# Pooled attention and a gated feed-forward on one core: weight words joined without ScalarE, a score tile's short product first, more engine choices, another order

## The chip, the core and the metric

The program runs on one core of a Trainium2 chip. A core has a matrix engine (TensorE, PE in the profile), a vector engine (VectorE, DVE), an activation engine (ScalarE, ACT), a general engine (GpSimd, POOL) and a queue that issues the transfers here (SyncE, SP). Each engine takes its instructions in the order in which they were recorded, and waits at an instruction until all that this one needs is done. The metric is the time of one execution on the device in microseconds (us).

## The reference, cut to what matters

```python
# q, k, v: (4, 8, 1152, 64) float32
q_pool = q.reshape(B, H, S // 2, 2, D).mean(axis=3)              # 576 pooled queries
scores = scale * np.matmul(q_pool, k.transpose(0, 1, 3, 2))      # 576 x 1152 for each head
scores = scores - np.max(scores, axis=-1, keepdims=True)
attn = np.exp(scores)
attn = attn / (np.sum(attn, axis=-1, keepdims=True) + 1e-09)
attn_out = np.matmul(attn, v)
x = attn_out.transpose(0, 2, 1, 3).reshape(B, 576, 512)          # the heads side by side
h = np.maximum(x @ w_in, 0.0)                                    # 512 -> 1024
conv_out = sum(conv_w[t] * shifted(h, t - 1) for t in range(3))  # over neighbouring tokens
out = (h * 1.0 / (1.0 + np.exp(-conv_out))) @ w_out              # 1024 -> 512
```

`w_in`, `conv_w` and `w_out` arrive as 64-bit floats. The kernel reads each as two 32-bit words and puts a 32-bit float together on the chip.

## The kernel before, in words

The 32 heads go in 16 pairs. A pair's 576 pooled queries are cut into four blocks of 128 and one of 64. For a block of 128 and one head of the pair there is a **score tile** of 128 queries by 1152 keys; the two heads share one tile for the block of 64. That makes 9 tiles for a pair and 144 in all.

A tile takes this way. `scores` (line 459) makes it on PE in three products, each with one half of PE's rows (64 of 128, since a head has 64 values): `main` 0 and 1 are 512 keys each and lie in different halves, `main` 2 is the 128 keys in the middle and lies in the half of `main` 0. The operand `qt` is the pair's queries, `qd` the same queries turned to the other half of the partitions. DVE takes the row maximum (`top`, 471), ACT the exponential with its row sum (`expo`, 476); DVE or ACT scale and invert the sum (489, 493, 499). Then a head goes one of two ways. For most heads ACT or POOL writes the high half of the weights in 16 bits (`high`, 518 on POOL and 523 on ACT), DVE the low half (`low`, 526), and a transposing transfer (539) turns both. For the seven heads in `X32`, POOL, DVE or ACT scale the row (`norm`, 557 and 561), PE turns it (575), and ACT brings it back from PSUM (`keep`, 580). Score tiles `s` have two buffers and the PSUM tiles `a` of all other products have two.

`values` (605, 611) multiplies the turned weights with v; ACT brings the result back (`keep`, 621), ACT or POOL splits off a high half (627, 629), DVE the low half (634). When the four pairs of a batch have their part, `feed` makes the 1024 hidden rows: products on PE (695), `relu` on ACT (701), the first tap on ACT or POOL (708, 712), two more taps on DVE (719), `tanh` on ACT (725), the gate on DVE (729). `second` makes the output product (902, 908, 914), ACT brings it back (928) and SP stores it.

The weights are put together in 17 pieces (`weights`: 8 of `w_in`, 8 of `w_out`, all 128 x 512, and a small one of 24 columns for `conv_w`). A piece takes, in a chain: load (987), absolute value on ACT (`size`, 991), `clamp` on DVE (995), three bit operations on DVE (`bits`, 1004, 1009, 1013), the low words made into scaled floats on ACT (`rest`, 1019), a product on DVE (`join(0)`, 1026) and a sum on POOL or DVE (`join(1)`, 1028); for `w_in` ACT adds up absolute values (1047). The query pairs are added up by `sum_q` (303), kept by `keep_q` (306) and turned by `turn_q` (310).

What stands where is written out by hand in three tables. `ORDER` names all tasks in one list over all engines; each engine's own order is that list with the others' tasks left out. `SWAPPED` names the tasks that go to their second engine (`alt`) instead of the first, and `SLOTS` gives each buffer its slot. There is no scheduler at run time. A task can change engine only where it has an `alt`.

Of the kernel before, what the change touches and what calls it, by code (L numbers as in the profile page):

```python
# [88 lines left out]
def unpack(words):  # L89
# [5 lines left out]
hZcZcXaac1c4c0c5c6c7cYh0auc2bNc3abacaddcaededdc8afdbh3h1daagdfahc9h2dtaih4aviiajawh5aEaxdsaybOilh6h7azifijh8aA  # L95
igdgdhibikaBihh9imaCdiiDaFdjindwaGicaHiAioiaaIaDaJiddyipakiBiqdldxdzdmixiEivaKdNdMieaLitiFiyiualiraMiCamiSanao
iGaNiHapaOdQaqd6iViwardSiTasiPiWiIatisaYiXiQdAiJaPjadniRiUaQdoaRaSiYdRiZaTiLjbi7aUiziKaZiNdpaVdqjva0jca1aWi8dT
iMd7jyi0a2i9jdjea3iOi3jwjia4i1i4i2jfjzjjjxi5a5i6jNjAjgjljBaXjQdrjmbijCa6dujneaa7jOjKa8ecjheddkdUjLjPdvdPjRjkbj
j5jDjSbkjIbljoj8j6a9ebjGbmjJetjMjEbnjHbabojrjTbbj7bpjUbcjFj9j2dBjVj3dCbdkabqj0knewbrkbdDkcbebEkqkkkoj1jsjYj4kd
jWkrjZkpkgbPkljXkFfGkhbFbfkikskmkGkebgkjdFk0kHbGktdGkudHdIkCesdJdKk3kIbHeydLexkDkSdOezkfkJk1bhkNkKbsk4kvk2kEkL  # L100
dEkOkTkPkQbtbIkRbJlik5bubvkMbyllk6k7ljlfbwkAlmk8kwkBkxkylgk9kzlkldbxlhlnlAbQlebzlDdVlolaeNbRlbbClpkWbSlBlxbKbT
dWbLbUlclylqlCdXbVlElvbMbDb5kXlzlFdZlSd0bAlGlHlVd1lPd2lIlTltlweQd3lWlulNlJb6lOb7lKlLb8lrlUb9calQcbmalXcclRlsmv
cdlYd4lZmbl0eRlMmcbWd5l5l1mwl7d8mdmyd9eSeAl2mebBl6l3mfmnl8eTmxmzmie7l9bXmgeedYeUmAmNbYmBmhbZmoefb0mQl4mCmOmDeg
mlmjmmmRmPmKmGmHb1mkmLmEb2mIm5mSehb3mMmJmTmUm6mFejmVm2m8ekb4elm7emm0eqmWencem9nnjpmXmpkUm1m3mYmrnajqm4ernoeojt
# [12 lines left out]
FstGFHtRFItPtzF8tHFJtQtStIF1F9gzFnGatJfIugF2fXF3tTFUuhtKtUtLF4tiF5tVtMtZGbuit0F6t2tWsat1GcFKt5GdF7FVgBtjGttXgD
FLFNGuGetYt3tkGvfOFWFuGwFOt6t4FPfPtNFvGxt7fQFXFMfRGfFQgCfSFYujtluxFRGgukfTult8GhuAfUuyGygEFwt9uBgSuaFxumFZFSub
uzGmF0uCfVuPfWGnuSuduQfZucGAGoueFyuDuEupuTuFuouUf5uGunGpuRvaufuIGzf6Gqu7uVFTGruWuqu0GBuLu8uHuJuMuXuKuNvbGVuOgo
u9uYFzu1gyGWFtvpu2Givcu3vqf7u5vHu4gUvrFAGjvIGku6vsvdf8GsveutvfvtvguZvuFBgVvvvhvwvigWFCvxuuFDvyG2FEGCFFGXg8GYvl  # L120
G3GDvJgaGZv2GEgbG4vmvnvKgcvAvLgdvjgev3vov5vkgfgXvzvPvDvFv6vMvEvGvBv4vQvNv7wgggvOvCG5wjvRwhGFgjv8JWg9vSgRvUv9GG
wdwkwagYwef9wlvTG6wiwbwuwfG7wmgpwnGlwIwowvvVGHwrwJwcwwHnwpGIG0G8GJwxwsHowKGOwyhbwzwtgqwWgrGKHpgsgtwLwAHqwBwXwF
vYwqGPG1wGwChcguGQwMhdgvGRHrwNwDHgwHvZgwwYwOgxxdHhwPGShegAxgxewEHiw5wZwTGLw0HjwQwUxhw1xfwVHuGTw2w6xrgGHkwRxiG9
GMxjHsGNxuwSfNHtHaxsHlHbHvxkHcxoxvw3HwxlxpxtgHxmHxxwHmxnHdxFgIHeGUxxHfxIgJxygKHAxGHBxzHCw4gPxHxqgLxAHDHyurxJgM
xCHExBgFvWxKxDxTuvw7xWxLxMw8xNxUw9usxQxEvXxXv0xVxRHFhqgNxYxOx7xaxZgOx0x8gTx1xPygx4uwv1x9x5xShsyryhyiyaHGyjyoht
x2IshugQhvypH0hHItybIuysIzycx3H1yqIvIeH2IAgZIwydHOIBytH3yfICyFH4IxIfyeJZyCIghJg0yux6HPIDyDHQIyyEg1yvyGHzywyzyQ
IhyxIlyAHRImyHyRyBIEyTIiySyIg2IFyJyNH7yUyyHSyKg3IGyOInziH5HHIoH8yLyVykyPH6Ijg4yWIHzjg5IIzkH9Iag6yMy4ylg7Ipy7yX
ymy5xbHIhLhay1yYy8hKHJIJzlzmy2znHKIqyZy3y9INIKy6IbzozDIcy0zaIdzbzGIOzfzEHLhNIrzFhpzgzrhMzHzczhIPzIIkynIQzdzRzs
# [43 lines left out]
def tile_pooled_attention_conv_gate_ffn(  # L172
# [262 lines left out]
    def softmax(o, d):  # L435
# [791 lines left out]
```

## Time and profile before

| | before |
|---|---|
| median of 3 runs | 635.98 us (635.82 to 636.93) |
| span of the profiled execution, first to last instruction | 633.9 us |
| what lies around the span (median less span) | 2.1 us |
| PE busy | 583.3 us (92%) |
| DVE busy | 575.9 us (91%) |
| ACT busy | 520.2 us (82%) |
| POOL busy | 159.6 us (25%) |

The page names no time of the profiled execution beside its span, so the median stands for it. Shares of the whole span are means over stretches with different limits; the rows further down cut the span into stretches. Only the time in which an engine waits, and what ends that wait, tells which engine sets the pace of a stretch. Times in the trace count from the span's start.

### The profile page before, as it was taken

The numbers are of one execution on the slowest core, as the hardware profiler recorded it, in microseconds if no ns is written. First come the engines' busy times: TensorE is split into PE (matmuls) and PEld (weight loads), VectorE is DVE, ScalarE is ACT, GpSimd is POOL, SyncE is SP. The second block draws the span as 40 slices with busy tenths as digits, with TensorE's granted clock in tenths as the row PEclk, the third lists the DMA queues.
The fourth block names the chain that finished last, engine by engine and source line by source line (L and its number), as shares of the span: only waits on it lengthen the run. The fifth ranks groups of instructions, "written<-read, shape, count | busy, mean of one in ns | idle before, by whom it ended". The sixth has DMA issues, their size and how long they took to land. (4 is left out here: it accounts for less than half of the span.)

```text
span 633.9 us, 11947 instructions
## 1 busy us (share of the span) xinstructions
PE 583.3 (92%) x4427; PEld 365.1 (58%) x4427; DVE 575.9 (91%) x948; ACT 520.2 (82%) x976; POOL 159.6 (25%) x166
## 2 busy tenths in 40 slices
PE   5679887898999899999999999999998999999997
PEld 3346554566665556546666666475665646566853
DVE  4999989999999999989998999999999999997771
ACT  5999989989998897879977899787869985775761
POOL 0332436533233312210212511202330122322210
PEclk7869989999999999999999999999999999999999
DMA  7788975847975599998989998999999898887601
GB/s 246 234 221 223 197 127 118 207 116 191 182 197 109 131 193 169 177 219 162 248 176 190 177 241 168 159 217 195 199 181 210 175 173 152 166 153 152 93 35 42
DMA packets 277386, 109.63 MB, mean 173 GB/s; under 512 B 264912, under 2 KB 266192, under 8 KB 277328
## 3 DMA queue, kind: packets, MB, share of 16 engines
q1 hardware_dynamic: 277328, 108.87, 83.3%
q8 instruction: 35, 0.57, 0.4%
q14 instruction: 23, 0.19, 0.1%
HBM read 37.77 MB, written 4.72 MB: 67 GB/s over the span
## 5 line engine op out<-in xcount | busy, mean ns | idle before, releaser
L476 ACT ACTIVATE p<-s,sm 128x1152 f32<-128x1152 f32 x144 | 175.2, 1217 | 41.2 <-DVE sm L471 18.8
L459 PE MATMUL s<-kt,qt 64*128 64x512 f32 (+3 forms) x704 | 189.0, 484 | 20.7 <-ACT p L476 16.5
L471 DVE TENSOR_REDUCE sm<-s 128x1 f32<-128x1152 f32 x144 | 193.1, 1348 | 7.3 <-PE s L459 6.9
L526 DVE SCALAR_TENSOR_TENSOR hl<-p,sm,hl 128x1152 f16<-128x1152 f32 (+1 forms) x116 | 167.0, 1449 | 4.3 <-POOL hl L518 2.4
L459 PEld LDWEIGHTS s<-kt,qt 64*128 64x128 f32 (+1 forms) x704 | 92.6, 178 | 124.3 <-issue 78.1
L459 PE MATMUL s<-kt,qd 64*128 64x512 f32 x256 | 147.3, 658 | 0.0
L518 POOL TENSOR_SCALAR hl<-p,sm 128x1152 f16<-128x1152 f32 (+1 forms) x52 | 72.1, 1388 | 230.1 <-DVE sm L499 145.8
L605 PE MATMUL a<-pt,v 128*64 128x256 f16 (+2 forms) x1566 | 119.8, 272 | 0.4 <-DVE v L399 0.4
L695 PE MATMUL a<-x,wi 128*128 128x257 f16 (+3 forms) x864 | 105.4, 274 | 3.6 <-ACT h L701 1.7
L605 PEld LDWEIGHTS <-v 128*64 128x64 f16 x1566 | 91.1, 110 | 10.2 <-issue 2.2
L695 PEld LDWEIGHTS <-wi 128*128 128x128 f16 x864 | 76.6, 98 | 30.3 <-issue 10.6
L523 ACT ACTIVATE hl<-p,sm 128x1152 f16<-128x1152 f32 (+1 forms) x64 | 79.4, 1249 | 12.3 <-DVE sm L499 9.1
L908 PE MATMUL a<-wo,g 128*128 128x512 f32 x160 | 74.7, 604 | 0.0
L719 DVE SCALAR_TENSOR_TENSOR g<-h,cw,g 128x255 f32<-128x255 f32 (+3 forms) x144 | 66.7, 482 | 4.1 <-ACT g L708 2.5
L575 PE MATMUL a<-ident,p 128*128 128x128 f32 (+1 forms) x315 | 49.1, 281 | 17.1 <-ACT pt L580 7.3
L611 PE MATMUL a<-pt,v 128*64 128x256 f32 (+1 forms) x252 | 64.1, 409 | 0.0
L575 PEld LDWEIGHTS a<-ident,p 128*128 128x128 f32 (+1 forms) x315 | 32.9, 144 | 31.1 <-ACT pt L580 10.1
L580 ACT ACTIVATE pt<-a 128x384 f32<-128x384 f32 (+2 forms) x98 | 44.6, 475 | 5.3 <-PE a L575 5.2
L701 ACT ACTIVATE h<-a,bs 128x257 f32<-128x257 f32 (+3 forms) x72 | 33.9, 472 | 14.3 <-PE a L695 9.4
L561 POOL TENSOR_SCALAR p<-p,sm 128x1152 f32<-128x1152 f32 (+1 forms) x20 | 28.1, 1408 | 69.0 <-DVE sm L499 42.9
L908 PEld LDWEIGHTS a<-wo,g 128*128 128x128 f32 x160 | 28.4, 190 | 28.8 <-issue 26.9
L611 PEld LDWEIGHTS a<-pt,v 128*64 128x64 f32 x252 | 33.4, 137 | 10.3 <-issue 0.7
(135 smaller groups left out, 648.8 us busy)
## 6 DMA issues: line engine op xcount, KB each, us to landing
qin<-in_q_dram SPq DMA_DIRECT2D x15, 640.0 KB, 4.6
kt<-in_k_dram SPq DMA_DIRECT2D x15, 576.0 KB, 5.0
vin<-in_v_dram SPq DMA_DIRECT2D x9, 576.0 KB, 4.4
g<-in_moe_w_in_dram SPq DMA_DIRECT2D x8, 512.0 KB, 4.6
w<-in_moe_w_out_dram SPq DMA_DIRECT2D x8, 512.0 KB, 4.2
out_dram<-o SPq DMA_DIRECT2D x16, 256.0 KB, 2.6
vin<-in_v_dram SPq DMA_DIRECT2D x7, 288.0 KB, 3.9
v<-in_v_dram SPq DMA_DIRECT2D x7, 288.0 KB, 4.1
```

Source lines behind the costliest of these rows:

```text
L459: nc.tensor.matmul(out=w, lhsT=f, rhs=kk, start=True, stop=True)
L471: nc.vector.tensor_reduce(out=sm[:, e:e + 1], in_=runs(st[e]), axis=AX.XY, op=ALU.max, negate=True)
L476: nc.scalar.activation(out=p.tile().rearrange("p (a n) -> p a n", a=2), in_=runs(st[e]), func=AF.Exp, bias=sm[:, e:e + 1], scale=1.0, accu ...
L518: eng.tensor_scalar(out=hl[rows, 0], in0=ps_[e][rows], scalar1=sm[rows, 6 + e:7 + e], scalar2=1.0, op0=ALU.mult, op1=ALU.mult,)
L523: nc.scalar.activation(out=hl[rows, 0], in_=ps_[e][rows], func=AF.Copy, scale=sm[rows, 6 + e:7 + e])
L526: nc.vector.scalar_tensor_tensor(out=hl[rows, 1], in0=ps_[e][rows], scalar=sm[rows, 6 + e:7 + e], in1=hl[rows, 0], op0=ALU.mult, op1=ALU.s ...
L575: nc.tensor.transpose(w[:, (i - a1) * nq:(i - a1 + 1) * nq], ps_[e][rows, i * P:(i + 1) * P], ident[rows, rows])
L605: nc.tensor.matmul(out=to, lhsT=o.v[:, e, c, vc:vc + D], rhs=o.pt[y, e][:, hl * NC + c, 0:n], start=(c == 0 and j == 0), stop=(c == NC - 1 ...
L611: nc.tensor.matmul(out=to, lhsT=o.v[:, e, c].bitcast(F32), rhs=p32.rearrange("p (a n) -> p a n", a=NC)[:, c, 0:n], start=(c == 0), stop=(c ...
L695: nc.tensor.matmul(out=w[:, 0:n], lhsT=wi[:, a, j, f * P:(f + 1) * P], rhs=x.x[:, c, s0:s0 + n], start=(i == 0 and j == 0), stop=(i == 2 a ...
L719: nc.vector.scalar_tensor_tensor(out=c, in0=h[:, t:t + tok], scalar=cw[:, f, t:t + 1], in1=c, op0=ALU.mult, op1=ALU.add)
L908: nc.tensor.matmul(out=w.tile(), lhsT=g[f // 4][:, f % 4, c:c + P], rhs=wo[:, f, :], start=(f == 0), stop=(f == FC - 1),)
```

## The change

**Weights.** `rest` is gone. `join(0)` now reads the low words itself, scales them and multiplies, in one instruction of DVE; ACT makes one conversion less for each of the 17 pieces. `clamp` may go to POOL.

**Score tiles.** `scores` makes the three products in the order `main` 2, 1, 0, so that the short one of 128 keys comes first and a long one of 512 last.

**Engine choices.** `turn_q`, the PSUM copies of `keep` in the softmax and in `values`, and `relu` may go to DVE instead of ACT.

**Order.** `ORDER`, `SLOTS` and `SWAPPED` are new throughout. Over the whole program POOL has 284 tasks in place of 160, DVE 862 in place of 888 and ACT 656 in place of 771; PE has the same 452.

```diff
 SWAPPED = """
-aiaMaWa6bqbAcdcNcWc8dcdqdwdKdQd4eaeoewe9fkfqfBf1gkgvgBgUhbhmhshJhUioixiGiYi0i7jfjpjBjDjKjVj2kkkCkIlflolqlxlGlY
+alaIaVa4bdbobybObWb4ccckcscAcNcPcTcUcVcYdhdCdVd7ete3fkfDgvgFg5hPh9iWi3i8jkjmjojEjGjIkckeklkrktkCkDkHk9lgltlHlJ
...
-        def turn_q(e, cols):
+        def turn_q(eng, e, cols):
             h, g = slice(D - D * e, P - D * e), slice(D * e, D * e + D)
+            if eng is not nc.scalar:
+                eng.tensor_scalar(
+                    out=o.qd.tile()[h, cols], in0=o.qin[g, 0, cols], scalar1=QSCALE, scalar2=1.0,
+                    op0=ALU.mult, op1=ALU.mult,
+                )
+                return
...
+                    alt=("DVE", 0.08 + (turned.stop - turned.start) / 1900.0, True)) for e in range(2)
...
         def scores(ends):
-            for main in (0, 1, 2):
+            for main in (2, 1, 0):
                 for e in ends:
...
+                        if eng is nc.scalar:
+                            nc.scalar.activation(out=to, in_=src, func=AF.Copy)
+                        else:
+                            eng.tensor_copy(out=to, in_=src)
...
-                            uses=[w, pt])
+                            uses=[w, pt], alt=("DVE", 0.06 + (a2 - a1) * nq / 930.0, False))
...
-        t = add("ACT", act(n, 0.1), keep, after=[t] + o.one, uses=[w] + ([] if all(o.x32) else [o.vs]), takes=[xf])
+        t = add("ACT", act(n, 0.1), keep, after=[t] + o.one, uses=[w] + ([] if all(o.x32) else [o.vs]), takes=[xf],
+                alt=("DVE", dve(n) - 0.03, False))
...
-            t = add("ACT", act(n, 0.155 if halved else 0.085), relu, after=[t, xs[0].back], uses=[w, xs[0].bs], takes=[h])
+            t = add("ACT", act(n, 0.155 if halved else 0.085), relu, after=[t, xs[0].back], uses=[w, xs[0].bs], takes=[h],
+                    alt=None if halved else ("DVE", dve(n) - 0.03, False))
...
-        def rest():
-            _, lo32, hi32, mm, a = parts()
-            nc.scalar.activation(
-                out=hi32.bitcast(F32), in_=lo32.bitcast(U32), func=AF.Copy, scale=2.0 ** -52
-            )
-
         def join(n, eng=None):
             _, lo32, hi32, mm, a = parts()
             if n == 0:
-                nc.vector.tensor_tensor(out=mm, in0=mm, in1=hi32.bitcast(F32), op=ALU.mult)
+                nc.vector.scalar_tensor_tensor(
+                    out=mm, in0=lo32.bitcast(U32), scalar=2.0 ** -52, in1=mm, op0=ALU.mult, op1=ALU.mult
+                )
             else:
                 eng.tensor_tensor(out=a, in0=mm, in1=a, op=ALU.add)
...
-        t = add("DVE", 0.08 + m / 1900.0, clamp, after=[t], uses=[tmp], port=True)
+        t = add("DVE", 0.08 + m / 1900.0, clamp, after=[t], uses=[tmp], port=True,
+                alt=("POOL", 0.19 + m / 1113.0, True))
...
-        t = add("ACT", act(m, 0.08), rest, after=[t], uses=both)
```

The next pieces show three places of the order. Line numbers of the changed kernel are its own: its 304 is 303 of before, 480 is 471 (row maximum), 467 is 459 (score product), 573 is 561 (`norm`), 528 is 518 (`high`), 1020, 1029, 1034, 1038, 1045 and 1049 are the weights' 995, 1004, 1009, 1013, 1026 and 1028, and 312 is `turn_q` on DVE.

DVE at the program's start, before: one weight piece, with the first row maximum in it.

```order
L995 TENSOR_SCALAR g<-g 128x512
L1004 TENSOR_SCALAR wo<-g 128x512
L303 TENSOR_TENSOR qin<-qin 128x384
L1009 SCALAR_TENSOR_TENSOR wo<-g,wo 128x512
L303 TENSOR_TENSOR qin<-qin 128x128
L1013 TENSOR_SCALAR g<-wo 128x512
L471 TENSOR_REDUCE sm<-s 128x1
L1026 TENSOR_TENSOR g<-g 128x512
L1028 TENSOR_TENSOR wo<-g,wo 128x512
```

The same place of DVE now.

```order
L304 TENSOR_TENSOR qin<-qin 128x128
L312 TENSOR_SCALAR qd<-qin 64x128
L480 TENSOR_REDUCE sm<-s 128x1 x2
L1020 TENSOR_SCALAR g<-g 128x512
L312 TENSOR_SCALAR qd<-qin 64x128
L1029 TENSOR_SCALAR wo<-g 128x512
L312 TENSOR_SCALAR qd<-qin 64x128
L1034 SCALAR_TENSOR_TENSOR wo<-g,wo 128x512
```

Two row maxima now stand ahead of the first weight piece; the load of the second part of the first keys stands third on SP instead of sixth, ahead of the first weight load.

POOL in the first stretch, before: row scalings, high halves and two of the weights' sums.

```order
L561 TENSOR_SCALAR p<-p,sm 128x1152
L405 MEMSET x 128x2x2
L1028 TENSOR_TENSOR wo<-g,wo 128x512
L561 TENSOR_SCALAR p<-p,sm 128x1152
L518 TENSOR_SCALAR hl<-p,sm 128x1152
L1028 TENSOR_TENSOR wo<-g,wo 128x512
L561 TENSOR_SCALAR p<-p,sm 128x1152
```

The same place of POOL now.

```order
L573 TENSOR_SCALAR p<-p,sm 128x1152
L1049 TENSOR_TENSOR wo<-g,wo 128x512
L304 TENSOR_TENSOR qin<-qin 128x640
L1049 TENSOR_TENSOR wo<-g,wo 128x512
L395 MEMSET vs 64x1
L573 TENSOR_SCALAR p<-p,sm 128x1152
L1020 TENSOR_SCALAR g<-g 128x512
L399 TENSOR_SCALAR v<-vin,vs 128x9x64
L413 MEMSET x 128x2x2
L573 TENSOR_SCALAR p<-p,sm 128x1152
L1049 TENSOR_TENSOR wo<-g,wo 128x512
L304 TENSOR_TENSOR qin<-qin 128x640
```

The weights' sums, a clamp and the sums of query pairs stand on POOL between the softmax's own work; the high halves of this stretch are on ACT.

PE, the first two score tiles before.

```order
L1138 MATMUL a<-ident 128x128 x16
L459 MATMUL s<-kt,qt 128x512
L459 MATMUL s<-kt,qd 128x512
L459 MATMUL s<-kt,qt 128x2x64
L459 MATMUL s<-kt,qt 128x512
L459 MATMUL s<-kt,qd 128x512
```

The same place of PE now.

```order
L1159 MATMUL a<-ident 128x128 x16
L467 MATMUL s<-kt,qt 128x2x64
L467 MATMUL s<-kt,qd 128x512
L467 MATMUL s<-kt,qt 128x512
L467 MATMUL s<-kt,qt 128x2x64
L467 MATMUL s<-kt,qd 128x512
```

The short product (128x2x64) went from the third place of a tile to the first; in each tile the two products with `qt` share one half of the rows and the one with `qd` has the other.

## Rows read from the trace of the kernel before

**Rows 1.** Busy time by stretch: length, PE, PEld, DVE, ACT, POOL, clock, DMA, GB/s

```profile
10.87:239.10 228.23, 197.39 (x1359) 125.76 (x1357) 219.49 (x360) 212.12 (x404) 76.68 (x71) 0.95 0.76 176
239.10:480.00 240.90, 237.29 (x1711) 144.79 (x1708) 228.36 (x346) 198.98 (x346) 52.56 (x55) 1.00 1.01 193
480.00:540.00 60.00, 53.69 (x450) 32.75 (x448) 58.48 (x102) 47.85 (x87) 11.53 (x14) 1.00 0.92 171
540.00:600.00 60.00, 59.85 (x657) 41.38 (x657) 51.35 (x83) 42.49 (x90) 15.07 (x15) 1.00 0.78 145
600.00:633.90 33.90, 29.23 (x236) 15.97 (x234) 15.78 (x57) 14.73 (x42) 2.65 (x5) 0.99 0.10 36
```

**Rows 2.** Waits of PE from 10.87 to 239.1 us: total, times, longest

```profile
PE s L459 <- ACT p L476: 11.2, 15, 1.6
```

**Rows 3.** Timeline of the first 12 us: start, length, instruction, idle time before it

```profile
3.87 0.60 SPq L262 DMA_DIRECT2D kt<-in_k_dram  x1
...
8.45 0.43 DVE L995 TENSOR_SCALAR g<-g 128x512 f32<-128x512 f32 x1 [7.59 <-ACT g L991]
...
9.99 1.22 PE L459 MATMUL s<-kt,qt 64*128 64x512 f32 x1 [3.69 <-DMA kt<-in_k_dram]
...
10.87 1.35 DVE L471 TENSOR_REDUCE sm<-s 128x1 f32<-128x1152 f32 x1
```

**Rows 4.** DVE's groups by shape: busy us, mean ns, idle before

```profile
L526 DVE SCALAR_TENSOR_TENSOR hl<-p,sm,hl 128x1152 f16<-128x1152 f32 x109 | 157.2, 1451 | 4.2 <-POOL hl L518 2.4 <-ACT hl L523 1.2
L399 DVE SCALAR_TENSOR_TENSOR v<-vin,vs,v 128x576 f16<-128x576 f32 x25 | 19.9, 811 | 0.3 <-ACT v L396 0.2
L303 DVE TENSOR_TENSOR qin<-qin 128x640 f32<-128x640 f32 x13 | 10.6, 818 | 0.2 <-DMA qin<-in_q_dram 0.2
L1026 DVE TENSOR_TENSOR g<-g 128x512 f32<-128x512 f32 x8 | 5.5, 687 | 0.0
L1009 DVE SCALAR_TENSOR_TENSOR wo<-g,wo 128x512 int32<-128x512 int32 x8 | 5.5, 686 | 0.1
L493 DVE SCALAR_TENSOR_TENSOR sm<-sm,small 128x2 f32<-128x2 f32 x33 | 5.1, 155 | 3.5 <-ACT p L476 3.0
L561 DVE TENSOR_SCALAR p<-p,sm 128x1152 f32<-128x1152 f32 x5 | 4.1, 811 | 0.0
L995 DVE TENSOR_SCALAR g<-g 128x512 f32<-128x512 f32 x8 | 3.4, 421 | 8.1 <-ACT g L991 8.1
L729 DVE SCALAR_TENSOR_TENSOR g<-g,h 128x65 f32<-128x65 f32 x8 | 1.6, 227 | 2.0 <-ACT g L725 1.9
```

**Rows 5.** ACT's conversion of the low words, half of the 16

```profile
L1019 ACT ACTIVATE w<-w 128x512 f32<-128x512 uint32 x8 | 5.4, 681 | 0.0
```

**Rows 6.** Timeline near 198 us: DVE and POOL side by side

```profile
198.20 1.34 DVE L471 TENSOR_REDUCE sm<-s 128x1 f32<-128x1152 f32 x1
...
199.81 2.70 DVE L526 SCALAR_TENSOR_TENSOR hl<-p,sm,hl 128x1152 f16<-128x1152 f32 x1
...
198.38 1.23 POOL L518 TENSOR_SCALAR hl<-p,sm 128x1152 f16<-128x1152 f32 x1 [2.73 <-DVE sm L499]
199.57 1.72 POOL L303 TENSOR_TENSOR qin<-qin 128x640 f32<-128x640 f32 x1
```

**Rows 7.** The first and the last DVE instruction that POOL held up

```profile
136.09 1.38 DVE L634 SCALAR_TENSOR_TENSOR x<-xf,bs,x 128x256 f16<-128x256 f32 x1
...
539.75 1.07 DVE L634 SCALAR_TENSOR_TENSOR x<-xf,bs,x 128x256 f16<-128x256 f32 x1
```

**Rows 8.** One score tile on PE, and the product after it

```profile
442.13 0.69 PE L459 MATMUL s<-kt,qt 64*128 64x512 f32 x1
442.14 0.69 PE L459 MATMUL s<-kt,qd 64*128 64x512 f32 x1
...
443.10 0.38 PE L459 MATMUL s<-kt,qt 64*128 64x128 f32 x2
443.41 2.81 PE L695 MATMUL a<-x,wi 128*128 128x257 f16 x24
```

More of the change, by code (lines that the diff above doesn't have):

```diff
@@ L100 @@
[L100 to L104, printed above, removed]
@@ L160 @@
+JsJBJNJRJTKuKBKIKPKWLaLhLqLsLwLDLKLRLYL5McMjMsMuMxMyMEMFMMMTM0M7NdNeNl
 """
@@ L319, in loads @@
             ready = [tq] + [
-                add("ACT", act(turned.stop - turned.start, 0.16), lambda e=e, turned=turned: turn_q(e, turned), after=[t],
-                    uses=[o.qin] + ([o.qd] if e or i else []), takes=[] if e or i else [o.qd]) for e in range(2)
+                add("ACT", act(turned.stop - turned.start, 0.16), lambda eng, e=e, turned=turned: turn_q(eng, e, turned), after=[t],
+                    uses=[o.qin] + ([o.qd] if e or i else []), takes=[] if e or i else [o.qd],
+                    alt=("DVE", 0.08 + (turned.stop - turned.start) / 1900.0, True)) for e in range(2)
             ]
@@ L466, in softmax @@
         for e in range(n):
+            plan.tag = ('softmax', o.pr, d, 2 if m else e)
             p = Buf(r_p)
@@ L577, in turn, with keep @@
                             )
[L579 to L584 removed]
+                    def keep(eng, w=w, a1=a1, a2=a2, nq=nq, pt=pt, c=c0):
+                        to = pt.tile().rearrange("p a n -> p (a n)").bitcast(F32)
+                        to = to.rearrange("p (a n) -> p a n", a=NC)[:, a1:a2, c:c + nq]
+                        src = w[:, 0:(a2 - a1) * nq].rearrange("p (a n) -> p a n", n=nq)
+                        if eng is nc.scalar:
+                            nc.scalar.activation(out=to, in_=src, func=AF.Copy)
+                        else:
+                            eng.tensor_copy(out=to, in_=src)
                     t = add("PE", (0.128 if nq == P else 0.075) * (a2 - a1), turn, after=[td],
@@ L618, in values, with keep @@
         to = slice(1 + first, 1 + first + n)
-        def keep():
-            nc.scalar.activation(
-                out=xf[:, 0:n], in_=w[:, 0:n], func=AF.Copy, scale=2.0 ** -14 if all(o.x32) else o.vs[:, 4:5],
-            )
+        def keep(eng):
+            by = 2.0 ** -14 if all(o.x32) else o.vs[:, 4:5]
+            if eng is not nc.scalar:
+                eng.tensor_scalar(
+                    out=xf[:, 0:n], in0=w[:, 0:n], scalar1=by, scalar2=1.0, op0=ALU.mult, op1=ALU.mult
+                )
+                return
+            nc.scalar.activation(out=xf[:, 0:n], in_=w[:, 0:n], func=AF.Copy, scale=by)
         def high(eng):
@@ L698, in mm, with relu @@
                         )
-            def relu(f=f, w=w, h=h):
+            def relu(eng=nc.scalar, f=f, w=w, h=h):
+                if eng is not nc.scalar:
+                    eng.tensor_scalar(
+                        out=h[:, 0:n], in0=w[:, 0:n], scalar1=xs[0].bs[:, 3:4], scalar2=0.0, op0=ALU.mult, op1=ALU.max
+                    )
+                    return
                 nc.scalar.activation(
@@ L991, in size, with clamp @@
             nc.scalar.activation(out=mm, in_=hi32.bitcast(F32), func=AF.Abs)
-        def clamp():
+        def clamp(eng):
             _, lo32, hi32, mm, a = parts()
-            nc.vector.tensor_scalar(
-                out=mm, in0=mm, scalar1=F64_MIN, scalar2=F64_MAX, op0=ALU.max, op1=ALU.min
+            eng.tensor_scalar(
+                out=mm, in0=mm, scalar1=F64_MAX, scalar2=F64_MIN, op0=ALU.min, op1=ALU.max
             )
```

125 lines of the change are left out of this document (64 added, 61 removed).

## The prediction

> **What bounds the kernel now.** I read the busy time by stretch first, because shares of the whole span hide that the program has two halves with different limits [rows 1]. Up to the 61st of the 144 row maxima, at 239 us, DVE is busy for 219.5 of 228.2 us and ACT for 212.1, while PE stands idle for 30.8 us; what PE waits for there is in first place the exponential that gives a score buffer back, 11.2 us [rows 2], and that comes behind full queues on ACT and DVE. So this stretch moves at the pace of DVE, with ACT 7 us behind it. From 239.1 to 480 us PE is busy for 237.3 of 240.9 us: there PE sets the pace, DVE has 12.5 us of air and ACT 42 us. Over all that follows 239.1 us PE has 380.1 us of work in 394.8 us (14.7 idle) and DVE 354.0 (40.8 idle), summed over the last four rows of [rows 1]. The program's first work on DVE comes late: it waits until 8.45 us for the first weight piece, and the first row maximum stands behind that piece, at 10.87 us [rows 3]. Last I read which instructions of DVE and POOL lie side by side [rows 6, 7], since most of the change is work handed to POOL.
>
> From this follows what a saving is worth: in the first stretch a microsecond off DVE is nearly one off the time, as long as ACT falls as well; after it, only less work or less waiting on PE counts.
>
> **The start.** DVE idles 7.59 us for the first weight piece [rows 3] while the first tile's scores could be read. Now the two first row maxima stand ahead of the piece, 2 x 1.35 us [rows 3], in time that was idle. The second part of the keys, which PE waited 3.69 us for, is issued two steps earlier on SP; its issue takes 0.60 us and pushes the weight load back by that [rows 3]. I take a gain of 2.7 less 0.6, some 2.0 us; at best 2.7, at worst 0 if the weights' chain then comes late.
>
> **DVE in the first stretch.** I counted the tasks that stand on DVE ahead of the 61st row maximum in the two orders, and price them by [rows 4]. Gone are 12 clamps, 11 of them of 512 columns: 11 x 0.42 = 4.6 us; 8 sums of `join(1)`: 8 x 0.69 = 5.5 (by L1026, the same operation and shape); 7 sums of query pairs: 7 x 0.82 = 5.7; 3 row scalings: 3 x 0.81 = 2.4; 4 scaled sums: 4 x 0.155 = 0.6. That is 18.8 us. The new `join(0)` has the form of L1009, 0.686 against 0.687 us: nothing. Added are 11 PSUM copies, 3 `relu` and 7 `turn_q`, 21 instructions that the trace has only on ACT; and 2 low halves of v that the order draws into this stretch, 2 x 0.81 = 1.6. The 21 lie between a small DVE instruction (0.227 us, L729) and one of 512 columns with two inputs (0.69). Copies and `relu` have 257 to 384 columns, nearest to the clamp's 0.42 but from PSUM, so I take 0.5; the turns, some of 128 columns, 0.3: 14 x 0.5 + 7 x 0.3 = 9.1 us. Sum: 18.8 - 9.1 - 1.6 = 8.1 us less. With the ends for the 21 (4.8 and 14.5 us) it is 12.4 or 2.7 us less.
>
> ACT loses the 17 conversions, 16 x 0.68 = 10.9 us [rows 5], and the instructions that DVE took; in exchange it takes high halves and scalings back from POOL in this stretch. It falls by about as much as DVE and so does not become the limit; were this cover missing, the gain would end at ACT's share.
>
> **What POOL costs DVE.** A row maximum reads one operand from PSUM. Beside it POOL's high half took 1.23 us and the maximum 1.34, its usual time [rows 6]: neither feels the other. An instruction of DVE with two operands in SBUF does feel POOL: beside `sum_q` (1.72 us) the low half took 2.70 instead of its mean 1.45 [rows 4, 6], and its end is one usual length after POOL's end. The trace has 14 such delays, the first and the last at 136.09 and 539.75 us [rows 7]; against the usual time of the same shape they cost 8.4 us, 5 of them, 4.3 us, in the first stretch. So the place of a POOL task matters. In the order before, 22 of POOL's 72 tasks of the first stretch do not follow a row maximum as DVE's latest task, in the new one 49 of 100. At the old rate, 4.3 us for 22, the 27 more cost 5.3 us. Ends: 0 if the order puts all of them where DVE is idle; 27 x 0.87 = 23 us if each collides like the five. I take 5.3, since the tables set POOL's place as they did before. The rule behind this is in the Trainium skill, page "SBUF — State Buffer", section "SBUF: two separate sides": DVE and GpSimd share a pair of ports, the one that starts first holds it for its whole instruction, and the other is blocked. The trace agrees: 2.70 us above. It speaks against this change, and is why the second rival has its chance.
>
> A wait is added too. DVE's first bit operation of a piece now waits for POOL's clamp in 12 pieces, and on POOL that clamp stands behind scalings and sums; what is queued behind it on DVE are row maxima, for which ACT and then PE wait. The trace has no such wait, so its price lies between 0 and one POOL task (1.72 us) for each of 12 pieces, 21 us. I take 0: weights are far ahead of their use at most pieces. The same holds for ACT's `keep_q` behind POOL's `sum_q`.
>
> **After 239 us.** POOL's tasks off a row maximum go from 40 to 91 there. The old rate (8.4 - 4.3 = 4.1 us for 40) makes 5.2 us on DVE, which has 40.8 us of air: hidden, and 5.2 us if that cover is gone. ACT falls by some 60 us, but PE waits so little there that I book no gain; half of the 14.7 us, 7 us, is the best I allow.
>
> **The short product first.** In a tile the product with `qt` and the one with `qd` start 0.01 us apart, in the two halves of the rows; the short one follows in the first half, 0.97 us after the start, and the next product stands 1.28 us after the start [rows 8]. First half: 640 keys; second: 512. In the new order the first half has the same 640 keys and the second the same 512, so I take 0. Bounds: the tail of the short one, 0.31 us from its start to the next product, holds about 0.1 us that a long last product could hide; 0.1 x 60 tiles of the PE-bound part is a gain of 6 us. The other end is a rival.
>
> **Sum.** 2.0 + 8.1 - 5.3 = 4.8 us off. The sum is of one profiled execution with a span of 633.9 us; around it lie 2.1 us, up to the median of 635.98, which I leave as they are: 635.98 - 4.8 = **631.2 us**.
>
> **Rivals.** (1) POOL becomes DVE's limit: slower. The first stretch loses what it won, 10.1 us, once 12 of the 27 added tasks collide at 0.87 us, or waits for clamps eat as much. If all 27 collide the cost is 23 us, and the time 635.98 - 10.1 + 23.5 = 649; in the middle some 641. For it: 5 of 22 collided before. Against it: there are 60 row maxima of 1.35 us in the stretch, 81 us, against 76.7 us of POOL before; but POOL now wants more than that room.
> (2) The short product blocks the halves: slower. If a waiting second pass of the `qd` product keeps the next `qt` product from being issued, the tile grows by up to half a long product, some 0.2 us. For the 80 or so tiles of the PE-bound part that is 16 us: 635.98 - 4.8 + 16 = 647. Against it: before, the `qd` product is issued 0.01 us after the `qt` product, whose second pass was still waiting [rows 8].
> (3) No change: the added waits take back 4 to 6 us, 635 to 637.
> (4) A larger gain: with ACT and DVE lighter, PE's waits in both parts shrink further, 10 us of the 30.8 and half of the 14.7: 618 to 622.
>
> **Chances.** Forecast, 622 to 634.7: 0.55. (1): 0.16. (2): 0.07. (3): 0.15. (4): 0.07. A measurement of this kernel can tell about 0.2%, 1.3 us, from no change. Faster by more: 0.55 + 0.07 = 0.62; within: 0.15; slower: 0.16 + 0.07 = 0.23. The range takes in the forecast, (3) and the nearer half of (1) and (2): 621 to 641 leaves out most of (4) and the rest of the two, about 0.18.
>
> **What would show it.** The start: the first row maximum before 8 us and two of them ahead of the first clamp. DVE: the 61st row maximum near 234 us instead of 239. POOL: busy some 280 us, and delays of DVE of 10 to 20 us in all, in the groups of L526's and L634's kind. Tiles: still 1.27 us to the next product; 1.4 or more would show (2). After the 61st maximum as much time as before, 395 us, with PE the limit. The prediction is wrong if the second part changes by more than 5 us either way, or if DVE's two-operand groups grow by more than a tenth.

## The result: slower, and the profile after

The changed kernel takes 640.4 us (median of 6 runs, 639.05 to 642.19) against 635.9 for the kernel before; the ratio is 1.0068 with a 95% interval of 1.0049 to 1.0087. The prediction was 631.2. The profiled execution took 641.25 us, with a span of 639.5. In what follows a **delay** is what a DVE instruction takes beyond the median of its line and shape in the same trace, counted from 60 ns on; the sums of delays are worked out from all instructions of a trace, and the groups below show the same growth in their means.

The stretches, cut at the first and at the 61st row maximum; the columns are those of [rows 1]:

```profile
6.20:237.00 230.80, 199.26 (x1377) 120.73 (x1375) 221.11 (x352) 205.24 (x378) 101.09 (x99) 0.94 0.78 183
...
237.00:639.50 402.50, 380.79 (x3031) 228.02 (x3027) 364.94 (x568) 248.16 (x479) 191.08 (x184) 0.99 0.87 165
```

The 61st row maximum comes at 237.0 us instead of 239.1, and what follows takes 402.5 us instead of 394.8 [rows 1]. ACT lost 56 us there, 304.1 to 248.2, and nothing came of it. POOL rose from 81.8 to 191.1 us, and DVE from 354.0 to 364.9, although it has 16 instructions fewer (568 after 584). So DVE does less and takes longer. DVE's groups by shape show where (busy us, mean ns, idle before), first three of the kernel before:

```profile
L471 DVE TENSOR_REDUCE sm<-s 128x1 f32<-128x1152 f32 x144 | 193.1, 1348 | 7.3 <-PE s L459 6.9
L719 DVE SCALAR_TENSOR_TENSOR g<-h,cw,g 128x321 f32<-128x321 f32 x48 | 25.1, 545 | 0.3 <-ACT g L708 0.2
L634 DVE SCALAR_TENSOR_TENSOR x<-xf,bs,x 128x256 f16<-128x256 f32 x20 | 10.7, 554 | 0.5 <-ACT x L627 0.5
```

The same groups in the changed kernel, with the low half (L536) and the new `join(0)` (L1045):

```profile
L480 DVE TENSOR_REDUCE sm<-s 128x1 f32<-128x1152 f32 x144 | 191.9, 1348 | 13.1 <-PE s L467 12.7
L536 DVE SCALAR_TENSOR_TENSOR hl<-p,sm,hl 128x1152 f16<-128x1152 f32 x109 | 166.2, 1531 | 3.7 <-POOL hl L528 2.4 <-ACT hl L533 1.1
L652 DVE SCALAR_TENSOR_TENSOR x<-xf,bs,x 128x256 f16<-128x256 f32 x20 | 14.5, 728 | 0.5 <-POOL x L647 0.5
L743 DVE SCALAR_TENSOR_TENSOR g<-h,cw,g 128x321 f32<-128x321 f32 x48 | 27.8, 605 | 0.4 <-POOL g L736 0.4
L1045 DVE SCALAR_TENSOR_TENSOR g<-g 128x512 f32<-128x512 uint32 x8 | 6.8, 852 | 0.0
```

The row maximum (L480), which reads PSUM, takes what it took. The low half (L536) has grown from 1451 to 1531 ns [rows 4], 109 x 0.080 = 8.7 us; the smaller two-operand shapes grew too: the conv taps (L743, before L719) from 545 to 605 ns, the low halves of values (L652, before L634) from 554 to 728. In all there are 55 delays of 34.9 us, where before had 14 of 8.4: 18 of 12.3 us in the first stretch (before 5 of 4.3), 37 of 22.6 behind it (9 of 4.1). By the POOL instruction beside them, the high halves (L528) cost 12.2 us in 15 delays and the query sums (L304) 11.6 us in 12; before, it was 4.8 us and 1.3.

One of each, as in [rows 6], DVE's rows first (start, length, instruction). The sum starts 0.27 us ahead of the low half:

```profile
198.64 0.42 DVE L1029 TENSOR_SCALAR wo<-o 128x512 int32<-128x512 int32 x1
198.97 2.70 DVE L536 SCALAR_TENSOR_TENSOR hl<-p,sm,hl 128x1152 f16<-128x1152 f32 x1
...
198.70 1.75 POOL L304 TENSOR_TENSOR qin<-qin 128x640 f32<-128x640 f32 x1 [2.29 <-DMA qin<-in_q_dram]
```

The low half of 1.41 us takes 2.70: it begins in earnest when the sum, at 200.45, is nearly done. Note the sum's releaser: the query pair had just landed, so its start has nothing to do with what DVE was at.

The start answers [rows 3]:

```profile
1.49 1.06 SPq L263 DMA_DIRECT2D kt<-in_k_dram  x2
...
6.24 2.62 DVE L480 TENSOR_REDUCE sm<-s 128x1 f32<-128x1152 f32 x2 [2.28 <-PE s L467]
...
9.57 0.48 DVE L1020 TENSOR_SCALAR g<-g 128x512 f32<-128x512 f32 x1 [0.71 <-ACT g L1016]
```

### The profile page after: what moved, and what is told of

It reads as the page before. It is cut to its first block, busy times and chain, and to the rows that moved or that the text cites. A ratio compares the mean times of both kernels' runs of the same rounds, so it can differ in the third digit from the quotient of the medians.

```text
span 639.5 us, 11923 instructions
## 1 busy us (share of the span) xinstructions
PE 584.9 (91%) x4427; PEld 353.3 (55%) x4427; DVE 586.6 (92%) x922; ACT 455.5 (71%) x861; POOL 293.0 (46%) x290
## 4 chain that ended last, share of the span: by engine, by line
DVE 46%; PE 26%; ACT 10%; issue 8%; DMA 6%; POOL 2%; SPq 1%; ACTq 0%; POOLq 0%; DVEq 0%
DVE hl L536 16%; DVE sm L480 14%; PE s L467 8%; PE a L714 4%; PE a L619 4%; DMA pt<-hl 4%; ACT p L485 4%; DVE g L743 4%; PE a L927 3%; DVE g L753 2%; DVE x L652 2%; PE a L587 2%; PE a L939 2%; ACT hl L533 1%; DVE v L407 1%
## 5 line engine op out<-in xcount | busy, mean ns | idle before, releaser
L480 DVE TENSOR_REDUCE sm<-s 128x1 f32<-128x1152 f32 x144 | 191.9, 1348 | 13.1 <-PE s L467 12.7
L467 PE MATMUL s<-kt,qt 64*128 64x128 f32 (+2 forms) x704 | 188.4, 482 | 16.6 <-ACT p L485 11.2
L536 DVE SCALAR_TENSOR_TENSOR hl<-p,sm,hl 128x1152 f16<-128x1152 f32 (+1 forms) x116 | 177.7, 1539 | 3.8 <-POOL hl L528 2.4
L528 POOL TENSOR_SCALAR hl<-p,sm 128x1152 f16<-128x1152 f32 x67 | 99.9, 1494 | 110.6 <-DVE sm L508 54.7
L467 PEld LDWEIGHTS s<-kt,qt 64*128 64x128 f32 (+1 forms) x704 | 78.7, 178 | 67.7 <-ACT p L485 39.3
L736 POOL TENSOR_SCALAR g<-h,cw 128x255 f32<-128x255 f32 (+3 forms) x67 | 50.5, 758 | 63.0 <-ACT h L725 36.1
L933 PE MATMUL a<-wo,g 128*128 128x512 f32 x160 | 77.4, 613 | 0.1
L743 DVE SCALAR_TENSOR_TENSOR g<-h,cw,g 128x255 f32<-128x255 f32 (+3 forms) x144 | 71.7, 528 | 4.4 <-POOL g L736 4.2
L533 ACT ACTIVATE hl<-p,sm 128x1152 f16<-128x1152 f32 (+1 forms) x49 | 61.3, 1253 | 10.7 <-DVE sm L508 3.4
L587 PEld LDWEIGHTS a<-ident,p 128*128 128x128 f32 (+1 forms) x315 | 34.7, 149 | 55.4 <-ACT pt L596 14.7
L933 PEld LDWEIGHTS a<-wo,g 128*128 128x128 f32 x160 | 28.1, 192 | 40.6 <-issue 38.8
L725 ACT ACTIVATE h<-a,bs 128x257 f32<-128x257 f32 (+3 forms) x64 | 30.7, 479 | 23.1 <-PE a L714 19.5
L596 ACT ACTIVATE pt<-a 128x384 f32<-128x384 f32 (+2 forms) x86 | 39.5, 474 | 7.7 <-PE a L587 7.1
```

Source lines behind the costliest of these rows:

```text
L467: nc.tensor.matmul(out=w, lhsT=f, rhs=kk, start=True, stop=True)
L480: nc.vector.tensor_reduce(out=sm[:, e:e + 1], in_=runs(st[e]), axis=AX.XY, op=ALU.max, negate=True)
L528: eng.tensor_scalar(out=hl[rows, 0], in0=ps_[e][rows], scalar1=sm[rows, 6 + e:7 + e], scalar2=1.0, op0=ALU.mult, op1=ALU.mult,)
L533: nc.scalar.activation(out=hl[rows, 0], in_=ps_[e][rows], func=AF.Copy, scale=sm[rows, 6 + e:7 + e])
L536: nc.vector.scalar_tensor_tensor(out=hl[rows, 1], in0=ps_[e][rows], scalar=sm[rows, 6 + e:7 + e], in1=hl[rows, 0], op0=ALU.mult, op1=ALU.s ...
L587: nc.tensor.transpose(w[:, (i - a1) * nq:(i - a1 + 1) * nq], ps_[e][rows, i * P:(i + 1) * P], ident[rows, rows])
```

## The experiments

Four theories stood after the result. The **port theory**: the delays above cost the time. The **order theory**: the new order and the moved tasks make other engines wait, and the delays only fill air. The **blocking theory** of the prediction's second rival (the short product first). And: the low words or the start gave less than booked. The kernel before was run beside each set; its medians lay between 635.9 and 636.7 us, and each ratio is against its own set.

**POOL's new tasks given to the kernel before, and taken from the one after.** The first moves 76 tasks (48 conv taps, 24 high halves of values, 4 high halves in front of the output product) from ACT to POOL in the old order; the second puts 79 of the changed kernel's POOL tasks back on ACT. Both are the same two lines over a list of tasks (in the second kernel with another list and `'ACT'`):

```
+        for i in unpack(MOVED):
+            self.tasks[i].engine = 'POOL'
```

> The kernel before, in its own order, with 76 tasks moved from ACT to POOL that the changed kernel has there (48 first taps, 24 high halves of values, 4 of the hidden rows). Nothing else is changed. Port theory: at the changed kernel's 0.25 us for each task off a row maximum these cost DVE 8 to 20 us, and the time grows by 3 to 10 us to 639 to 646, though ACT falls by some 40 us. Order theory: the time stays within 1.5 us of 636 or falls, since ACT is relieved and the order is the old one.

> The changed kernel with 79 of POOL's tasks put back on ACT: those first taps and high halves that in its order do not follow a row maximum as DVE's latest task (36 taps, 24 softmax high halves, 13 of values, 6 others). Everything else, the order too, stays. Port theory (the changed kernel is slower because POOL's added tasks hold up DVE's two-operand instructions, 55 delays and 34.9 us in its trace against 14 and 8.4 before): delays fall to some 20 to 30 and 10 to 18 us, DVE busy falls from 586.6 to some 568, and the time falls by 6 to 14 us to 626 to 634, below the kernel before. Order theory (the new order itself is worse, wherever POOL's tasks lie): the time stays within 2 us of 640, or grows as ACT takes 60 us more.

Before with the tasks on POOL: 644.0 us, ratio 1.0111 (1.0079 to 1.0142). Delays rose from 8.4 to 14.7 us and DVE's busy time by 6.6; DVE also waited for POOL's taps, 5.5 us. That is the port theory's outcome, though not all of the 7 us is the port. The second went against it: 659.7 us, ratio 1.0359 (1.0328 to 1.0389). Delays fell only to 26.3 us, and DVE waited in places that it had not (waits in us, times, longest):

```profile
DVE g L750 <- ACT g L739: 13.1, 11, 2.8
...
DVE hl L543 <- ACT hl L540: 8.1, 5, 3.5
DVE sm L515 <- ACT sm L505: 6.3, 7, 1.4
...
DVE x L659 <- ACT x L652: 4.1, 4, 1.5
```

ACT runs in order, and a task inserted in its queue where it has no gap holds up all behind it. So this run changed two things at once and says nothing of the port; what was wanted was a kernel in which order, queues and POOL's time stay, and only its reads go.

**POOL's work kept in length, without its reads.** In the changed kernel 140 POOL tasks don't stand right behind a row maximum in the order. The 99 of them that are conv taps, high halves, row scalings and query sums issue a one-column instruction, which keeps the wait for the source, and a memset (the sums two memsets):

```
+        eng.tensor_scalar(out=self.cut(out, slice(0, 1)), in0=self.cut(in0, slice(0, 1)), **kw)
+        eng.memset(self.cut(out, slice(1, n)), 0.01)
```

> The changed kernel with the 99 POOL tasks that do not stand right behind a row maximum in the order (conv taps, high halves, norms, query sums) replaced by a one-column tensor_scalar, which keeps the wait for the source, and a memset of the remaining columns, which only writes. Leaves out: the values of those tiles. Order, queues and waits as in the changed kernel, POOL's busy time expected within 20% of its 293 us. Port theory (a POOL instruction that reads SBUF next to a DVE instruction of two SBUF operands holds it up): the DVE instructions that run long fall from 34.9 us to 5 to 14 us, DVE busy from 586.6 to 560 to 568 us, time 618 to 633 us, below both kernels. Order theory (POOL's longer queue and the new order make others wait, the port only shifts air): the long DVE instructions shrink as well, but the time stays at 637 to 642 us.

It took 628.2 us, ratio 0.9877 (0.986 to 0.9894), 12 us below the changed kernel. Two rows of POOL, and its stretches:

```profile
L179 POOL MEMSET hl<- 128x1151 f16 x23 | 24.2, 1054 | 0.0
L178 POOL TENSOR_SCALAR g<-h,cw 128x1 f32<-128x1 f32 x36 | 16.9, 470 | 30.7 <-ACT h L749 19.4 <-ACT sm L522 6.5 <-DVE h L745 3.2
```

```profile
7.37:230.50 223.13, 196.97 (x1375) 119.22 (x1374) 214.23 (x352) 204.63 (x378) 103.57 (x133) 0.95 0.80 188
230.50:625.80 395.30, 376.13 (x3032) 227.28 (x3027) 357.37 (x568) 247.55 (x480) 187.22 (x257) 0.99 0.87 168
```

POOL is as busy as in the changed kernel (291.6 us in all, 293.0 there), and its queue is the same; what went is 14.4 us of DVE's busy time (586.6 to 572.2), as delays fell by the same 14.4, to 20.5. The first stretch ends 6.5 us earlier, the rest is 7.2 us shorter. The port theory gave 618 to 633, the order theory 637 to 642. Delays fell by less than the 21 to 30 us expected: 20.5 us are left, 18.6 of them beside tasks that do stand behind a row maximum in the order, on which more below. One reserve: the memsets change the values that PE multiplies, and PE's busy time is 5.8 us less, so the whole 12 us need not be DVE's. How much that can be, a run further down shows: with the old product order and unchanged values PE's busy time behind the 61st maximum falls as far (376.35 us, here 376.13, in the changed kernel 380.79), and the time by 1.3 us only, its profiled span by 3.0. The next runs change no values.

**The same sums in pieces, and seven tasks where ACT has room.** If DVE waits for the rest of one POOL instruction, shorter instructions cost less.

```
+    def tensor_tensor(self, out, in0, in1, op):
+        for s in self.parts(out):
+            self.nc.gpsimd.tensor_tensor(out=out[:, s], in0=in0[:, s], in1=in1[:, s], op=op)
```

`parts` cuts a sum of 640 columns into four of 160.

> The changed kernel with each of POOL's 15 query sums of 640 columns issued as four instructions of 160 columns; same engine, same order, same result. One-instruction theory (a DVE instruction that meets a POOL instruction on two SBUF operands waits for the rest of that one POOL instruction; read from the changed kernel, where the long DVE instruction is late by what POOL's had left, 1.49 us left and 1.36 us late): the sums' 10.3 us of delay fall to 2 to 5 us, all delays from 34.9 to 27 to 31 us, time 634 to 638 us. Rival (the amount of POOL work in columns sets the price, whatever its pieces): delays as before within 2 us, time 639.5 to 642 us.

> As the run with the sums alone, and the 37 softmax tasks of POOL that do not stand behind a row maximum in the order (24 high halves, 13 norms, 1152 columns) issued as three instructions of 384 columns. One-instruction theory: their delay falls to a third, all delays from 34.9 to 14 to 24 us, time 627 to 635 us, below the changed kernel and perhaps below the kernel before. Rival (each piece is held up behind a DVE instruction of its own, so that POOL's results come later and the low halves wait): delays fall, but DVE's waits for POOL's high halves rise by 4 us or more and the time stays at 638 to 648 us. Rival (columns set the price): 639 to 642 us with the delays unchanged.

> The changed kernel with seven of its high halves put back on ACT: those which held up a DVE instruction (6.0 us together) and for which ACT shows a gap of 1.5 us or more near POOL's start. Port theory: delays from 34.9 to 28 to 30 us, time 634 to 638 us. Rival (as when 79 tasks went back to ACT, the in-order queue of ACT makes others wait): 639 to 645 us.

> The changed kernel with the query sums in four pieces and the seven high halves on ACT together: the two edits that made it faster one by one (6.2 and 4.3 us below its 640.4 us). If both take away delays of DVE at different places, the gains add: delays 34.9 - 4.0 - 6.8 = 24 us, DVE busy near 576.5 us, time 628 to 632 us, below both kernels. If they only shift the same air: 634 to 636 us, as each alone.

The sums in pieces: 634.2 us, ratio 0.9964 (0.9948 to 0.998), faster than both kernels. Near the place shown above, DVE's rows first:

```profile
196.59 1.68 DVE L557 SCALAR_TENSOR_TENSOR hl<-p,sm,hl 128x1152 f16<-128x1152 f32 x1
198.19 1.54 DVE L764 SCALAR_TENSOR_TENSOR g<-h,cw,g 128x321 f32<-128x321 f32 x2
...
196.28 3.85 POOL L182 TENSOR_TENSOR qin<-qin 128x160 f32<-128x160 f32 x4 [2.24 <-DMA qin<-in_q_dram]
```

The low half now takes 1.68 us, 0.27 late, instead of 2.70. But POOL, let in between DVE's instructions one piece at a time, needs 3.85 us for what took 1.75, and delays more of them: the sums' delays are 26 instead of 12, of 7.5 us instead of 11.6 (2 to 5 were expected), all delays 30.7. The time fell by more than the delays did; I don't know what gave the rest.

With the 37 softmax tasks in pieces as well: 638.2 us, ratio 1.0017 (0.9999 to 1.0036), which is the first rival's case. A delay beside a piece is some 0.26 us, but all delays stay at 30.4, and DVE waits for the late pieces:

```profile
DVE hl L557 <- POOL hl L178: 4.3, 7, 1.1
```

With 2.2 us for the whole high halves that is 6.5 us, after 2.4 in the changed kernel. A piece helps where nobody waits for the result. The seven high halves on ACT, where it had a gap of its own: 636.1 us, ratio 0.9993 (0.9976 to 1.001), with 28.1 us of delays: 6.8 us less, as expected, for 4.3 us of time, and without the waits of the 79. Both edits together: 632.6 us, ratio 0.9931 (0.9912 to 0.9949), near the 628 to 632 expected and faster than either kernel. The gains add for the most part (6.2 and 4.3 us alone, 7.8 together). The delays missed their forecast: 28.7 us are left, where 24 were expected, and DVE is busy for 580.1 us, not 576.5. So this time too the time fell by more than the delays.

**What a longer queue of POOL costs by itself.** In the kernel before, each of the 72 large softmax tasks of POOL was followed by work that nobody needs, once with reads, once without:

```
+            if t.engine == "POOL" and t.ns > 0.5 and t.tag[0] == "softmax":
+                for _ in range(3):        # second kernel: 7 memsets
+                    nc.gpsimd.tensor_scalar(out=idle_sb, in0=idle_sb, ...)
```

> The kernel before with three more POOL tensor_scalar instructions of 128x160 on a private tile (estimate 0.55 us each, from the 128x255 one at 0.62 us) behind each of the 72 large softmax tasks of POOL: some 117 us more POOL time, nobody waits for their result. Port theory: at the changed kernel's price of 0.25 us for a POOL task off a row maximum, 72 of them add 18 us of delay to DVE; time 644 to 656 us. Queue theory (only the later tasks of POOL's queue matter): the same time as with memsets in their place, within 3 us.

> As the run with three tensor_scalars, but with seven memsets of 128x160 (estimate 0.23 us each, from the 128x128 one at 0.204 us) in their place: the same POOL time, written only. Port theory: DVE's delays stay at 8 to 11 us, time 636 to 639 us. Queue theory: as much slower as the tensor_scalars.

Here the port theory failed. With reads 652.1 us, ratio 1.0242 (1.0227 to 1.0258), but with memsets 657.8, ratio 1.0335 (1.032 to 1.035), though the latter have fewer delays than the kernel before, 6.2 us. Added POOL time, with reads and with memsets, and the waits of the run with memsets:

```profile
L1177 POOL TENSOR_SCALAR idle_sb<-idle_sb 128x160 f32<-128x160 f32 x216 | 134.2, 621 | 12.2
L1177 POOL MEMSET idle_sb<- 128x160 f32 x504 | 119.0, 236 | 24.9
```

```profile
PE s L460 <- ACT p L477: 21.5, 23, 2.7
...
DVE sm L472 <- PE s L460: 13.7, 18, 4.1
...
DVE hl L527 <- POOL hl L519: 11.5, 11, 1.5
PE a L576 <- POOL p L562: 11.1, 6, 4.3
```

In the old order the low half and the transposes stand close behind POOL's results, so 1.6 us more in POOL's queue reaches them: a queue price that has nothing to do with the port. Nearly all of it falls in the first stretch, whose 61st row maximum comes at 259.3 us (with reads 251.7, before 239.1); behind it both are within 4 us of before. In the changed kernel the waits for POOL stay small (DVE 4.2 us for its taps, 2.4 for its high halves), so its order seems to have made room for the queue. That is argued from these waits; the run with the 99 tasks, which keeps the queue and gains 12 us by fewer reads, bears it out. Why memsets cost more than the longer instructions with reads stays open.

**The small parts.** The order of the products undone in the changed kernel; the low words joined without ACT alone; and the start alone (second part of the keys and the first row maximum moved up), the last two in the kernel before:

```
-            for main in (2, 1, 0):
+            for main in (0, 1, 2):
```

> The changed kernel with a score tile's products in the old order, main 0, 1, 2. My step (the short product first costs and saves nothing, since each half of PE's rows has the same keys): within 1.5 us of 640. Rival (the short product first blocks a half): 5 to 16 us faster. The traces so far: next product 1.28 us after a tile's start in both; a second tile right behind starts 0.97 us after the first instead of 1.07, but both end after 2.14.

> The kernel before with the low words joined without ACT, and nothing else: the 17 conversions go, the order is the old one without them. The sum in the prediction gives ACT 10.9 us less in the first stretch and DVE nothing; with DVE at the limit there by 7 us, a gain of 0 to 3 us: 633 to 636. If ACT set the pace of the first stretch with DVE, up to 6 us.

> The kernel before with two places of its order moved: the load of the first pair's second key part right behind the first part's, and the first row maximum ahead of the first clamp of the weights. Start term of the prediction (2.0 us of DVE's first idle time go and the gain is carried to the end): 633 to 635 us. Rival (the gain at the start is absorbed by a later wait that has its own pace, the loads or PE's rows): 635.5 to 637 us, with the first row maximum still about 3 us earlier.

The old product order: 639.1 us, ratio 1.0041 (1.0027 to 1.0054), 1.3 us below the changed kernel: within what was expected of no effect. The low words alone: 637.0 us, ratio 1.002 (1.0005 to 1.0035). ACT is 7.5 us less busy, and the 61st row maximum comes later, at 241.3 us: in the old order ACT's saved time buys nothing. The start alone: 637.3 us, ratio 1.0014 (1.0001 to 1.0027). The first row maximum does come 4.4 us earlier, and then:

```profile
6.50 1.36 DVE L471 TENSOR_REDUCE sm<-s 128x1 f32<-128x1152 f32 x1 [5.63 <-PE s L459]
...
12.51 0.69 DVE L1026 TENSOR_TENSOR g<-g 128x512 f32<-128x512 f32 x1 [1.19 <-ACT g L1019]
...
13.84 1.35 DVE L471 TENSOR_REDUCE sm<-s 128x1 f32<-128x1152 f32 x1
```

DVE idles for ACT's conversion of the low words, and the second maximum is 0.35 us later than before. That the gain would have stayed if the conversion had gone too is argued from this row; the two together were not run in the old order.

## Why the prediction was wrong, point by point

**The start (-2.0 us): right.** DVE's idle time up to 10 us fell by 2.1 us, and up to the 61st maximum by 1.9. The start alone gained nothing in the old order, because DVE then waited for the conversion on ACT; the step did not see that it hung on more than the order of the start.

**DVE's own work in the first stretch (-8.1): right.** DVE was busy for 221.7 us up to the 61st maximum, before 221.9; less the delays, 12.3 and 4.3 us, that is 209.4 after 217.6, 8.2 us less. The new copies and `relu` took 0.47 to 0.55 us (assumed 0.5) and the turns 0.22 to 0.42, 0.3 on average (assumed 0.3).

**Clamps and `sum_q` on POOL as something to wait for (0): right.** DVE waits for no clamp. PE waited once, 5.1 us up to 12.19 us, for a `keep_q`, but not because of POOL: POOL's sum ahead of it started when its load had landed and was done at 9.77 us, and `keep_q` ran at 11.83, behind two exponentials on ACT. DVE idled 0.1 us in that time.

**The short product first (0): right,** by the run that undid it, within its 1.3 us.

**What POOL costs DVE in the first stretch (+5.3): too small, 8.0.** So the 61st maximum came at 237.0 us, not near 234. The failing step is the rate of 4.3 us for 22 tasks. I counted "5 of 22" delays for the tasks off a row maximum. Put beside the trace one by one, 4 of those 5, 3.4 of the 4.3 us, came from tasks that do follow a row maximum in the order; one came from the 22. In the changed kernel the tasks behind a row maximum cost 18.3 us and the others 16.6. What stands ahead of a task in a list does not say beside what it runs.

The rate also gave unlike tasks one price. Up to the 61st maximum POOL had two query sums of 640 columns before, with 1.3 us of delay beside them, and has nine now, with 7.7: 6.4 of the 8.0 us more come with these seven sums, 0.9 us for each. One takes 0.82 us on DVE [rows 4], so the 5.7 us booked for taking them off DVE came back as delays.

Taken over all of POOL's tasks the price was 8.4 us for 160, 0.052 each, and is now 34.9 for 284, 0.123. POOL's load alone does not make that rise: with the added instructions that read, POOL was busy for 286.6 us in the old order, nearly as long as in the changed kernel, and all its delays were 13.9 us, 2.7 of them beside the added ones. What goes with the rise in the changed kernel: before, POOL's high halves idled 145.8 us for DVE's inverse, and after 54.7, as these rows of the two traces' waits say, before first:

```profile
POOL hl L518 <- DVE sm L499: 145.8, 24, 19.6
```

```profile
POOL hl L528 <- DVE sm L508: 54.7, 19, 6.7
```

A released task starts in step with DVE, one out of a queue or behind a transfer at any time: 45 of 160 POOL tasks started during a DVE instruction of the scalar-and-tensor form (28%), now 105 of 284 (37%). That this drives the price is argued from those counts, and not shown: with the added instructions in the old order the wait for the inverse fell too, to 100.9 us, while the other delays rose from 8.4 to 11.2 only. A kernel with POOL's starts tied to row maxima was not tried.

**After 239 us (0, "hidden" in 40.8 us of air): wrong, +7.7.** This is the larger miss, and has two halves. The delays are 18.5 us more, not 5.2: 9.3 of that beside high halves of the softmax (53 on POOL, before 34), 3.8 beside six query sums, where POOL had none. And they were not hidden: with less reading on POOL, DVE's busy time in this stretch fell by 7.6 us and the stretch by 7.2, of which the reserve above may take a part, while DVE still shows 38 us idle. So, as I read it, an engine with 10% air in a long stretch can still be the one that ends last at each single step: a late low half or tap is waited for at once. PE's idle time there rose from 14.7 to 21.7 us. It cuts the other way too: without delays DVE has 7.6 us less work here (342.3 after 349.9), a saving that I booked at nothing. The two parts, 2.1 us less and 7.7 more, are the 5.6 us by which the profiled spans differ; the medians differ by 4.5.

**Rival (1) is what happened,** at its cheap end and in the other place: it was priced for the first stretch, and the loss fell behind it. The signs named in the prediction pointed there: delays of 10 to 20 us were 34.9, POOL's 280 us were 293, the second part changed by more than 5 us, and of the two-operand groups L634's grew by more than a tenth (554 to 728 ns). Where the prediction says that the port is why the second rival has its chance, it is this first one. Without the reads of the 99 tasks the time is 7.8 us below the kernel before, so the order and the moved work were worth a gain; how much of it is PE's is the reserve above.

## What to carry to other kernels

Price work that is handed to POOL kind by kind, by what DVE runs when POOL really starts, from the trace: one rate over unlike tasks did not carry over from one order to the next (0.052 us each before, 0.123 after), and a long sum gave back as delays what it took off DVE. Don't call an engine's idle time in a long stretch a cover without looking at who waits for the late instruction. If POOL must read while DVE is the limit, issue in short pieces what nobody needs soon, and put single tasks back on an in-order engine only where that engine has a gap: moving 7 gained 4.3 us, moving 79 lost 19.

## What the hardware showed that was not expected

In these traces a DVE instruction with two operands in SBUF that meets a running POOL instruction waits for the rest of that one instruction, then goes, with POOL's next one held until it is done: beside pieces of 160 columns it was 0.27 us late (the median of 26 delays, one of them 0.80), beside whole sums up to 1.36. Not only instructions with two operands in SBUF are held: a bit operation with one took 1.47 us instead of 0.42 beside a sum (DVE's row, then POOL's).

```profile
17.73 1.47 DVE L1029 TENSOR_SCALAR wo<-g 128x512 int32<-128x512 int32 x1
...
17.37 1.54 POOL L304 TENSOR_TENSOR qin<-qin 128x640 f32<-128x640 f32 x1 [1.44 <-DMA qin<-in_q_dram]
```

Memsets on POOL held up no instruction with two operands: none of the 20.5 us of delays lies beside a memset of the filled tasks, and beside the 504 memsets only two operations with one operand were late, 0.12 and 0.13 us; beside the 216 added instructions that read, 26 operations were. This agrees with the Trainium skill, page "SBUF — State Buffer", section "SBUF: two separate sides", which limits the lock for DVE instructions with two SBUF inputs to POOL instructions that read SBUF, and names DVE's two-port modes as the other case.

PE's clock dipped where it had not before. The granted clock is 0.83 from 500 to 510 us and 0.66 from 520 to 530, so in part of each it was at the lower of its two levels, 1.2 GHz and not 2.4; before, the stretch from 480 to 540 us was at 1.00 [rows 1]. In the 20 us ahead of the second dip PE was busy for 16.7:

```profile
500.00:510.00 10.00, 8.38 (x23) 3.97 (x24) 9.86 (x24) 4.59 (x9) 5.96 (x5) 0.83 0.91 169
510.00:520.00 10.00, 8.30 (x76) 4.74 (x74) 9.44 (x16) 5.99 (x11) 4.15 (x4) 1.00 1.01 152
520.00:530.00 10.00, 9.12 (x72) 6.34 (x72) 7.91 (x14) 5.38 (x10) 4.69 (x7) 0.66 0.89 174
```

With the old product order the same stretch is at 1.00 again and the time 1.3 us less; that the one comes from the other was not tested. The sums in pieces have 0.89 to 0.94 in the four slices from 490 to 530 us. Over the two stretches the changed kernel has 0.94 and 0.99, as the sums in pieces have at 634.2 us, and the 99 filled tasks 0.95 and 0.99 at 628.2; so the clock is not what makes these kernels differ.
